# Block transposes for a third batch, later scores, and a new order of the opening, in a fused attention and two-FFN kernel

## The chip, the cores and the metric

The kernel runs on one core of a Trainium2 chip. Its metric is the device time of one execution in microseconds. A run of the kernel before took 1285.98 us in the median of three (1285.95 to 1286.9). The profiled execution is another one, and took 1288.85 us.

## The reference

```
scores = x @ state.T / 8        # per batch (8) and head (8); x 512 x 64, state 32 x 64
xread  = softmax(scores) @ state
scores2 = state @ x.T / 8
sread  = softmax(scores2) @ x
x  = concat(xread, sread)       # 544 tokens a batch, 512 wide, heads side by side
h  = relu(x @ w_in);  y = (h * h) @ w_out          # 512 -> 2048 -> 512
out = ((y @ w1) * (y @ w2)) @ w3 @ w_out2          # 512 -> 1024 -> 1024 -> 512
```

x and state come as float32, the six weights as float64 words, and the output is float32 (4352 x 512). The two softmaxes run over different axes of the same 512 x 32 scores.

## The kernel before

All large products run in float32r. Each operand is kept as a rounded high part and the rest (HI, LO; `split`, L80 to L85: the high part by ScalarE, the rest by a VectorE subtraction), and a product is three matmuls, `PASSES`. The weights are converted from float64 words by integer work: `convert64` (L132) is five VectorE instructions of 128 x 512 and one of ScalarE. A raw weight tile is one of three buffers (`raw`, L110) and is loaded three conversions ahead; `conv()` (L557) converts the next one and loads another.

xread @ w_in is computed as a product with state @ w_in: `make_sw(b, fg)` (L408) multiplies the state of batch b by a group of four 128-column blocks of w_in, by sixteen narrow matmuls into two banks. An h tile (c, f) (`h_tile`, L434) is then six matmuls of `sw` and the transposed softmax `aT`, and `y_tile` (L469), called two steps later, multiplies the squared tile by w_out, twelve matmuls into four banks y0 to y3 that stay open over a segment of f. At a segment's end the four banks are copied out and stored (L485 to L490).

The main loop (L631) steps through 16 f for each of 8 batches c, and then the state rows (c = 8). For c = 0 and 1 the steps are interleaved in segments of f (0 to 3 of batch 0, 0 to 3 of batch 1, 4 to 7 of batch 0, and so on). A step, with index i, is called a slot here. In slot i, h_tile is followed by the jobs of `side[i]` (conversions, loads, `make_sw`), a y_tile, and the jobs of `late[i]` (attention of a later batch). These lists are written by hand. Within them the planner of the language orders each engine's instructions by their place in the program and by when it reckons that their inputs are there. `tc.issue_after(ins)` keeps what a block issues on the engine of `ins`, and on no other engine, behind `ins`.

Attention of batch b (`att_steps`, L267) needs x twice: with d on the partitions for the scores (`xT`), and as it is for sread (`X`). For b < `BLK` (3), `load_x` and `make_x` load and copy X, `xpose` turns it by sixteen TensorE transposes, and `soft1a` and `a_T` turn scores and softmax by eight transposes each into banks of the pool `bank_m`, which has two buffers. For b >= BLK, `load_xb` (L240) loads x in pieces of 32 floats by eight DMAs for each half g, `turn_x` (L253) turns 32 x 32 blocks on VectorE, `soft1a` and `a_T` do the same with scores and softmax, and `load_xn` (L260) loads X. These batches hold a raw tile from `load_xb` to `turn_x`, and their output rows are in another order (L887). `att_slots` (L389) says in which of the 16 slots of the batch before each step of the attention comes.

The opening (L513 to L542) loads state and x, turns x, computes scores and softmax of batch 0, converts the first half of w_in's first group and makes `sw` and `aT` of batch 0. Its last step is `first`, the VectorE subtraction that ends the split of the second `aT`. The jobs of `side[0]` that VectorE does are issued behind it.

Of the kernel before, what the change touches and what calls it, by code (L numbers as in the profile page):

```python
# [8 lines left out]
F32 = mybir.dt.float32  # L9
# [3 lines left out]
ACTF = mybir.ActivationFunctionType  # L13
# [7 lines left out]
def kernel(  # L21
# [17 lines left out]
    nc = tc.nc  # L39
# [6 lines left out]
    P = 128  # L46
    G = 2
    HG = H // G
    J = S // P
    NF = DF // P  # L50
# [3 lines left out]
    NT9 = B * NS  # L54
    scale = 1.0 / float(D) ** 0.5
    HI, LO = 0, 1
    BLK = 3

    def f32(ap):
        return ap.bitcast(F32)  # L60
# [1 line left out]
    const = ctx.enter_context(tc.tile_pool(name="const", bufs=1))  # L62
# [6 lines left out]
    ebias = const.tile([P, 1], F32, name="ebias")  # L69
    nc.vector.memset(ebias, -896.0 * 2.0**23)  # L70
    def bank_m(name):
        return psum.tile([P, 512], F32, tag="m", bufs=2, name=name)
# [4 lines left out]
    def bank_y(d, name):  # L77
        return psum.tile([P, 512], F32, tag=f"y{d}", bufs=1, name=name)
# [88 lines left out]
    def load_win0(half, kk, early):  # L167

        cols = slice(half * 256, (half + 1) * 256)
        load64(("win0", half, kk), [w_in[k * P:(k + 1) * P, cols] for k in (2 * kk, 2 * kk + 1)], early)  # L170

    def make_win0(half, kk):
        if win_t[0] is None:
            win_t[0] = wpool.tile([P, ND, 512], F32, tag="wi0", bufs=2, name="win0")
        convert64(("win0", half, kk), win_t[0][:, 2 * kk:2 * kk + 2, half * 256:(half + 1) * 256])
# [10 lines left out]
    def make_wout(f):  # L186
        w = att.tile([P, 512], F32, tag="cw", bufs=2, name="cw")
        convert64(("wo", f), w)

        def halves():  # L190
            t = wpool.tile([P, 2, DM], F32R, tag="wo", bufs=NF, name=f"wo{f}")
            split(t[:, HI], t[:, LO], w)
            wo_t[f] = t

        open_splits.append(halves)
# [24 lines left out]
    def load_x(b, g, early=False):  # L220
        t = raw_tile(early, f"x{b}_{g}").bitcast(F32).rearrange("p a b -> p (a b)")
        nc.sync.dma_start(
            t.rearrange("p (h k) -> p h k", h=HG),
            x[b, g * HG:(g + 1) * HG].rearrange("h (p j) d -> p h (j d)", j=J),
        )
        raws["x", b, g] = t.rearrange("p (h j d) -> p j h d", h=HG, j=J)

    def make_x(b, g, engine, early=False):

        pool, tag, bufs = (wpool, "wo", NF) if early else (att, "X", 2)  # L230
        t = pool.tile([P, J, HG, D], F32, tag=tag, bufs=bufs, name=f"X{b}_{g}")
        if engine is nc.scalar:
            nc.scalar.copy(t, raws.pop(("x", b, g)))
        else:
            engine.tensor_copy(t, raws.pop(("x", b, g)))
        X[b, g] = t
# [30 lines left out]
    def att_steps(b):  # L267
# [45 lines left out]
        def soft1a(r):  # L313
            e = att.tile([P, J * HG, NS], F32, tag="e2" if b == 0 and r else "e1", bufs=1, name="e1")
            if b >= BLK:
                nc.vector.transpose(out=e.rearrange("p k n -> p (k n)"), in_=v["S", r])
# [20 lines left out]
        def a_T(r):  # L337
            e = v["e1", r].rearrange("p k n -> p (k n)")
            if b >= BLK:
                ps = v["S", r]  # L340
                nc.vector.transpose(out=ps, in_=e)
            else:
                ps = bank_m("ps_a")
                for j in range(J):
                    nc.tensor.transpose(ps[:, j * P:(j + 1) * P], e[:, j * P:(j + 1) * P], ident)
            t = pa.tile([P, 2, 512], F32R, tag=f"aT{r}", bufs=2, name=f"aT{r}")
            aT_t[b, r] = t
            return split(t[:, HI], t[:, LO], ps)
# [40 lines left out]
    def att_slots(b):  # L389
        if b >= B:  # L390
            return [[] for _ in range(NF)]
        xp, sc, s2, s1a, s1b, at, a2t, sr, srt = att_steps(b)
        if b >= BLK:
            return [
                [sc], [], [s2[0], s1a[0]], [],
                [s1b[0], s2[1]], [a2t[0]], [at[0], s1a[1]], [sr[0]],
                [s1b[1], srt[0]], [a2t[1]], [at[1]], [sr[1]], [srt[1]], [], [], [],
            ]
        return [
            [xp[0]], [xp[1]], [xp[2]], [xp[3]],  # L400
            [sc], [s2[0]], [a2t[0]], [s1a[0], s2[1]],
            [sr[0], s1b[0]], [srt[0]], [a2t[1], at[0]], [sr[1], s1a[1]],
            [srt[1], s1b[1]], [at[1]], [], [],
        ]

    SW = {}

    def make_sw(b, fg, cols=slice(0, 512)):  # L408
        pss = [bank_m("ps_sw") for _ in range(G)]
        for k in range(HG):  # L410
            for r in range(G):
                rows = slice(r * D, (r + 1) * D)
                nc.tensor.matmul(  # L413
                    pss[r][k * NS:(k + 1) * NS, cols], stT[rows, b, k, :], win_t[fg][rows, k, cols],
                    start=True, stop=True, tile_position=(r * D, k * NS),
                )
        for r in range(G):
            if (b, fg, r) not in SW:
                SW[b, fg, r] = pa.tile([P, 2, 512], F32R, tag=f"sw{r}", bufs=2, name=f"sw{r}")
            t = SW[b, fg, r]  # L420
            split(t[:, HI, cols], t[:, LO, cols], pss[r][:, cols])
# [73 lines left out]
    def load_st(half):  # L495

        t = raw_tile(True, f"st{half}").bitcast(F32).rearrange("p a b -> p (a b)")[:, :B * D]
        t = t.rearrange("p (b r d) -> p b r d", r=2, d=D)
        for k in range(HG):
            for r in range(G):  # L500
                (nc.sync if half else nc.scalar).dma_start(
                    t[k * NS:(k + 1) * NS, :, r, :],
                    state[half * (B // 2):(half + 1) * (B // 2), 2 * k + r].rearrange("b n d -> n b d"),
                )
        st.append(t.rearrange("p b r d -> p b (r d)"))

    def make_st(half):
        ps = bank_m("ps_st")
        for k in range(4):
            nc.tensor.transpose(ps[:, k * P:(k + 1) * P], st[half][:, k, :], ident)  # L510
        nc.scalar.copy(stT[:, 4 * half:4 * half + 4].rearrange("p b k n -> p (b k n)"), ps)

    load_st(0)  # L513
    load_x(0, 0, True)
    load_x(0, 1, True)
    load_win0(0, 0, True)
    make_x(0, 0, nc.vector)
    make_x(0, 1, nc.scalar)
    load_win0(0, 1, True)
    load_win0(1, 0, True)  # L520
    load_win0(1, 1, True)
    load_wout(0, True)
    for g in range(G):
        load_x(1, g, True)
    load_st(1)
    for g in range(G):
        make_x(1, g, nc.scalar, True)
    make_st(0)
    xp, sc, s2, s1a, s1b, at, a2t, sr, srt = att_steps(0)
    xp1, sc1, s21, s1a1, s1b1, at1, a2t1, sr1, srt1 = att_steps(1)  # L530
    for step in xp:
        step()
    sc()
    make_win0(0, 0)
    make_win0(0, 1)
# [2 lines left out]
    s1b[0]()  # L538
    at[0]()
    s1b[1]()  # L540
    make_sw(0, 0, slice(0, 256))
    first = at[1]()  # L542

    convs = [("win", 1, k) for k in range(ND)] + [("wo", f) for f in range(4, 8)]
    convs += [("win", 2, k) for k in range(ND)] + [("wo", f) for f in (8, 9)]
# [25 lines left out]
    def sw(b, fg):  # L571
        return lambda: make_sw(b, fg)

    side = {i: [] for i in range(NF * B)}
    late = {}
    side[0] = [lambda: make_win0(1, 0), s2[0], lambda: make_win0(1, 1), xp1[0], xp1[1], a2t[0]]
    side[1] = [lambda: make_sw(0, 0, slice(256, 512)), lambda: make_wout(0), xp1[2], xp1[3], sr[0], s2[1], sc1]
    side[2] = [conv, s1a1[0], srt[0], a2t[1], s1b1[0], sr[1], at1[0]]
    side[3] = [conv, s21[0], srt[1], s1a1[1], a2t1[0], conv, s1b1[1], sw(1, 0), at1[1]]
    side[4] = [conv, s21[1], sr1[0], lambda: make_st(1)]  # L580
    side[5] = [conv, a2t1[1], srt1[0]]
    side[6] = [conv, conv, sr1[1]]
# [7 lines left out]
    for b in range(2, B):  # L590
        for i, steps in enumerate(att_slots(b)):
            late[(b - 1) * NF + i] = steps
        for fg in range(NFG):
            if (b, fg) != (B - 1, NFG - 1):
                side[b * NF + 4 * fg + 1].append(sw(*((b, fg + 1) if fg + 1 < NFG else (b + 1, 0))))
        for g in range(G):
            i = 9 + g if b == 2 else (b - 2) * NF + 12 + g
            if b < BLK:
                side[i].append(lambda b=b, g=g: (load_x(b, g), make_x(b, g, nc.scalar)))
            else:  # L600
                side[i - 4].append(lambda b=b, g=g: load_xb(b, g))
                side[i - 2].append(lambda b=b, g=g: turn_x(b, g))
                side[i + 2].append(lambda b=b, g=g: load_xn(b, g))
# [266 lines left out]
    def out_tile(c, t, s):  # L870
# [15 lines left out]
        if c < B:  # L886
            rows_t = "(p j) e -> j p e" if c < BLK else "(j p) e -> j p e"  # L887
            dst = out[c * T:c * T + S, :].rearrange(rows_t, j=J)[t]
# [97 lines left out]
```

## Time and profile before

| what | value |
|---|---|
| profiled execution | 1288.85 us |
| span, first to last instruction | 1287.0 us |
| TensorE busy | 1253.1 us, 97% |
| VectorE busy | 798.0 us, 62% |
| ScalarE busy | 655.1 us, 51% |
| mean granted TensorE clock | 0.993 |
| TensorE granted half clock | 22.13 to 32.38 and 39.20 to 46.03 us |

Busy is the share of the span in which an engine has an instruction under way. The ends of matmuls are modelled, so a TensorE that waits a little between matmuls can be shown as busy; the spacing of the h tiles shows this better. PE is TensorE, DVE VectorE, ACT ScalarE, SP the engine that issues nearly all DMAs; SPq and ACTq are their issue queues.

### The profile page before, as it was taken

What the parts mean: (1) busy time and instruction counts of PE and PEld (TensorE: products, weight loads), DVE (VectorE), ACT (ScalarE), POOL (GpSimd) and SP (SyncE); (2) the same over time, 40 slices, a digit from 0 to 9 for tenths busy, and PEclk for the clock granted to TensorE, in tenths of its full rate; (3) what the DMA queues carried; (4) which work ended last, traced back from release to release, by engine and by line L of the source; (5) the groups of instructions that cost most, each with busy time, mean ns of one, the idle gap of its engine ahead of it and who ended that gap; (6) DMA issues with size and microseconds to landing.
All of it is one profiled execution on the core that took longest, in us unless ns stands there. A gap on an engine that the chain in (4) does not pass through costs nothing.

```text
span 1287.0 us, 16895 instructions
## 1 busy us (share of the span) xinstructions
PE 1253.1 (97%) x6392; PEld 986.7 (77%) x6392; DVE 798.0 (62%) x1444; ACT 655.1 (51%) x1174; POOL 23.3 (2%) x22
## 2 busy tenths in 40 slices
PE   4899999999999999999999999999999999999998
PEld 2566677677777777777789888888888888778877
DVE  4998965868577575753243763746465656666652
ACT  4776765657566565655555543535353442424231
POOL 0000000000000000000000000000510000000000
PEclk8899999999999999999999999999999999999999
DMA  6146525454453634510222531021530415050323
GB/s 212 43 151 202 179 80 118 105 123 144 95 163 76 162 114 113 151 49 34 73 91 66 174 108 46 37 95 61 172 116 29 154 59 178 27 188 26 106 66 99
DMA packets 122962, 137.94 MB, mean 107 GB/s; under 512 B 71425, under 2 KB 75009, under 8 KB 122369
## 3 DMA queue, kind: packets, MB, share of 16 engines
q1 hardware_dynamic: 121728, 136.61, 35.0%
q8 instruction: 50, 0.82, 0.3%
q10 hardware_dynamic: 1152, 0.26, 0.1%
q14 instruction: 32, 0.25, 0.1%
HBM read 93.32 MB, written 43.52 MB: 106 GB/s over the span
## 4 chain that ended last, share of the span: by engine, by line
PE 88%; DMA 4%; DVE 3%; ACT 3%; issue 1%; SPq 0%; ACTq 0%; DVEq 0%
PE y L480 26%; PE po L876 14%; PE qa L795 10%; PE qd L795 7%; PE qc L795 3%; PE ps_w L680 3%; PE qe L795 3%; PE ps_sw L413 2%; DMA yscr<-yo 2%; PE ab L850 2%; PE ps_r L362 1%; DMA x<-in_x_dram 1%; PE ps_s L290 1%; DVE sw L85 1%; PE ps_w L665 1%
## 5 line engine op out<-in xcount | busy, mean ns | idle before, releaser
L480 PE MATMUL y<-ghl,wo 128*128 128x512 f32 (+1 forms) x1728 | 406.6, 381 | 3.2 <-DVE yo L487 1.5
L480 PEld LDWEIGHTS y<-ghl,wo 128*128 128x128 f32 x1728 | 308.5, 188 | 93.9 <-ACT r L428 18.4
L85 DVE TENSOR_TENSOR ghl<-r,ghl 128x512 fp32r<-128x512 f32 (+1 forms) x144 | 94.9, 659 | 162.1 <-ACT ghl L84 161.2
L795 PE MATMUL qa<-yq,wq 128*128 128x512 f32 x576 | 146.3, 390 | 0.7 <-ACT s L803 0.7
L795 PEld LDWEIGHTS qa<-yq,wq 128*128 128x128 f32 x576 | 107.6, 188 | 24.8 <-ACT s L803 1.8
L803 ACT COPY s<-qa 128x512 f32<-128x512 f32 x96 | 56.1, 587 | 138.3 <-PE qa L795 127.4
L795 PE MATMUL qd<-yq,wq 128*128 128x512 f32 x384 | 98.3, 390 | 0.0
L876 PE MATMUL po<-w34b,c 128*128 128x512 f32 x408 | 95.8, 391 | 0.3 <-DVE o L885 0.3
L876 PE MATMUL po<-w,c 128*128 128x512 f32 x408 | 95.2, 390 | 0.0
L876 PEld LDWEIGHTS po<-w34b,c 128*128 128x128 f32 x408 | 75.7, 188 | 18.1 <-DVE c L85 1.0
L430 ACT ACTIVATE r<-r 128x512 f32<-128x512 f32 (+1 forms) x144 | 87.5, 608 | 3.2
L876 PEld LDWEIGHTS po<-w,c 128*128 128x128 f32 x408 | 75.6, 188 | 17.3 <-DVE c L85 0.8
L84 ACT CAST ghl<-r 128x512 fp32r<-128x512 f32 (+1 forms) x144 | 85.8, 596 | 3.8 <-PE y L480 0.5
L795 PEld LDWEIGHTS qd<-yq,wq 128*128 128x128 f32 x384 | 71.8, 188 | 15.7 <-ACT s L803 1.0
L129 ACT ACTIVATE ce<-ce,ebias 128x512 int32<-128x512 int32 x72 | 52.1, 725 | 48.5 <-DVE ce L128 48.4
L807 DVE TENSOR_TENSOR s<-qa,s 128x512 f32<-128x512 f32 x32 | 22.1, 691 | 75.2 <-ACT s L803 75.2
L84 ACT CAST c<-s 128x512 fp32r<-128x512 f32 x64 | 39.6, 621 | 37.1 <-DVE s L824 36.7
L84 ACT CAST yq<-yraw 128x512 fp32r<-128x512 f32 x70 | 42.6, 622 | 24.6 <-DVE yraw L770 15.5
L885 DVE TENSOR_TENSOR o<-po,opart 128x512 f32<-128x512 f32 x34 | 23.3, 688 | 45.4 <-PE po L876 34.5
L85 DVE TENSOR_TENSOR yq<-yraw,yq 128x512 fp32r<-128x512 f32 x70 | 46.6, 682 | 5.4 <-ACT yq L84 5.1
L795 PE MATMUL qc<-yq,wq 128*128 128x512 f32 x192 | 49.5, 390 | 0.0
L152 DVE SCALAR_TENSOR_TENSOR ce<-raw,ce 128x512 int32<-128x512 int32 x72 | 49.1, 683 | 0.3 <-ACT ce L129 0.3
(548 smaller groups left out, 1812.4 us busy)
## 6 DMA issues: line engine op xcount, KB each, us to landing
raw<-in_moe_w_dram SPq DMA_DIRECT2D x32, 512.0 KB, 4.6
yraw<-yscr SPq DMA_DIRECT2D x56, 256.0 KB, 5.3
raw<-in_moe_w_out_dram SPq DMA_DIRECT2D x24, 512.0 KB, 4.0
yscr<-yo SPq DMA_DIRECT2D x48, 256.0 KB, 3.0
oscr<-o SPq DMA_DIRECT2D x34, 256.0 KB, 2.2
opart<-oscr SPq DMA_DIRECT2D x34, 256.0 KB, 3.2
out_dram<-o SPq DMA_DIRECT2D x32, 256.0 KB, 3.0
raw<-in_moe_w_in_dram SPq DMA_DIRECT2D x12, 512.0 KB, 3.9
```

The lines of the kernel that those rows point to most:

```text
L84: nc.scalar.copy(hi, src)
L85: return nc.vector.tensor_tensor(out=lo, in0=src, in1=f32(hi), op=ALU.subtract)
L129: nc.scalar.activation(e, e, ACTF.Relu, bias=ebias, scale=8.0)
L152: nc.vector.scalar_tensor_tensor(out=e, in0=hw, scalar=-(2**31), in1=e, op0=ALU.bitwise_and, op1=ALU.bitwise_or)
L413: nc.tensor.matmul(pss[r][k * NS:(k + 1) * NS, cols], stT[rows, b, k, :], win_t[fg][rows, k, cols], start=True, stop=True, tile_position=( ...
L430: nc.scalar.activation(r[:, :n], r[:, :n], ACTF.Square)
L480: nc.tensor.matmul(y_ps[c, d][:, :n], wo_t[f][:, wi, d * P:(d + 1) * P], t[:, gi, :n], start=(f == f0 and k == 0), stop=(f == f1 - 1 and k ...
L680: nc.tensor.matmul(ps, t[:, wi, (j % 4) * P:(j % 4 + 1) * P], wo2_t[j][:, vi, :], start=(j == 0 and k == 0), stop=(j == N1 - 1 and k == 2),)
L795: nc.tensor.matmul(ps, W[w, kt][:, wi, m * P:(m + 1) * P], Y[v, kt][:, vi, :], start=(first and kt == 0 and k == 0), stop=(last and kt == ...
L803: nc.scalar.copy(t, ps)
L850: nc.tensor.matmul(pss[i][:, :NT9], w[:, wi, m * P:(m + 1) * P], Y[B, d][:, vi, :NT9], start=(d == 0 and k == 0), stop=(d == ND - 1 and k ...
L876: nc.tensor.matmul(ps, v[:, vi, t * P:(t + 1) * P], w[:, wi, :], start=(m == 0 and k == 0), stop=(m == QM - 1 and k == 2),)
```

## The change

- `BLK` goes from 3 to 2, so batch 2 goes by block turns, too. Its blocks are loaded in slots 14 and 15, turned in 16 and 17, and X is loaded in 20 and 21 (before: load and copy in 9 and 10).
- For b >= BLK the scores move from the first of the 16 slots to the third, the steps behind them by one slot.
- In the opening all loads go by SP, in the order x of batch 0, a pair of weight loads, half of the state, the rest. A small exponential at the start (`warm`) needs nothing that is loaded. Both halves of x are copied by VectorE, and the state is turned behind x.
- The softmax's `a_T` of batch 0 and the first `make_sw` take banks of the y group instead of `bank_m`.
- The copies of batch 1's x (`make_x`, ScalarE) come behind `first` in the program, in an `issue_after(first.ins)` block.
- In `side[0]` to `side[3]`, `a2t[0]`, `sr[0]`, `srt[0]` and `sr[1]` come later, and `s2[0]` behind both conversions.

```diff
-    BLK = 3
+    BLK = 2
...
-                ps = bank_m("ps_a")
+                ps = bank_m("ps_a") if b else bank_y(2 + r, "ps_a")
...
-                [sc], [], [s2[0], s1a[0]], [],
-                [s1b[0], s2[1]], [a2t[0]], [at[0], s1a[1]], [sr[0]],
-                [s1b[1], srt[0]], [a2t[1]], [at[1]], [sr[1]], [srt[1]], [], [], [],
+                [], [], [sc], [s2[0], s1a[0]],
+                [], [s1b[0], s2[1]], [a2t[0]], [at[0], s1a[1]], [sr[0]],
+                [s1b[1], srt[0]], [a2t[1]], [at[1]], [sr[1]], [srt[1]], [], [],
...
-    def make_sw(b, fg, cols=slice(0, 512)):
-        pss = [bank_m("ps_sw") for _ in range(G)]
+    def make_sw(b, fg, cols=slice(0, 512), banks=None):
+        pss = [banks(r, "ps_sw") if banks else bank_m("ps_sw") for r in range(G)]
...
-                (nc.sync if half else nc.scalar).dma_start(
+                nc.sync.dma_start(
...
+    warm = const.tile([P, 1], F32, name="warm")
+    nc.scalar.activation(warm, ebias, ACTF.Exp, scale=0.0)
+    for g in range(G):
+        load_x(0, g, True)
+    load_win0(0, 0, True)
     load_st(0)
-    load_x(0, 0, True)
-    load_x(0, 1, True)
-    load_win0(0, 0, True)
-    make_x(0, 0, nc.vector)
-    make_x(0, 1, nc.scalar)
     load_win0(0, 1, True)
+    for g in range(G):
+        make_x(0, g, nc.vector)
...
-    for g in range(G):
-        make_x(1, g, nc.scalar, True)
-    make_st(0)
...
     for step in xp:
         step()
+    make_st(0)
     sc()
...
-    make_sw(0, 0, slice(0, 256))
+    make_sw(0, 0, slice(0, 256), bank_y)
     first = at[1]()
+    with tc.issue_after(first.ins):
+        for g in range(G):
+            make_x(1, g, nc.scalar, True)
...
-    side[0] = [lambda: make_win0(1, 0), s2[0], lambda: make_win0(1, 1), xp1[0], xp1[1], a2t[0]]
-    side[1] = [lambda: make_sw(0, 0, slice(256, 512)), lambda: make_wout(0), xp1[2], xp1[3], sr[0], s2[1], sc1]
-    side[2] = [conv, s1a1[0], srt[0], a2t[1], s1b1[0], sr[1], at1[0]]
-    side[3] = [conv, s21[0], srt[1], s1a1[1], a2t1[0], conv, s1b1[1], sw(1, 0), at1[1]]
+    side[0] = [lambda: make_win0(1, 0), lambda: make_win0(1, 1), s2[0], xp1[0], xp1[1]]
+    side[1] = [lambda: make_sw(0, 0, slice(256, 512)), lambda: make_wout(0), xp1[2], xp1[3], a2t[0], s2[1], sc1]
+    side[2] = [conv, s1a1[0], sr[0], a2t[1], s1b1[0], srt[0], at1[0]]
+    side[3] = [conv, s21[0], sr[1], srt[1], s1a1[1], a2t1[0], conv, s1b1[1], sw(1, 0), at1[1]]
...
-            i = 9 + g if b == 2 else (b - 2) * NF + 12 + g
+            i = (b - 2) * NF + (18 if b == 2 else 12) + g
             if b < BLK:
                 side[i].append(lambda b=b, g=g: (load_x(b, g), make_x(b, g, nc.scalar)))
             else:
```

The lines behind the `else` are unchanged: `load_xb` in slot i - 4, `turn_x` in i - 2, `load_xn` in i + 2.

## Rows read from the trace of the kernel before

**Rows 1.** The page, part 1: busy us (share of the span) xinstructions.

```profile
PE 1253.1 (97%) x6392; PEld 986.7 (77%) x6392; DVE 798.0 (62%) x1444; ACT 655.1 (51%) x1174; POOL 23.3 (2%) x22
```

**Rows 2.** Windows, the first 10 us: busy us (x) by engine, clock, DMA share, GB/s.

```profile
0.00:10.00 10.00, 0.00 (x0) 0.00 (x0) 0.75 (x2) 1.79 (x2) 0.70 (x6) 1.00 0.83 238
```

**Rows 3.** Timeline, opening: start us, us, engine, line, operation [idle before, releaser].

```profile
0.74 7.43 ACTq L501 DMA_DIRECT2D st<-in_state_dram  x8
0.74 0.40 SPq L121 DMA_DIRECT2D raw<-in_moe_w_out_dram  x1
...
6.90 0.69 DVE L235 COPY X<-x 128x1024 f32<-128x1024 f32 x1 [6.04 <-DMA x<-in_x_dram]
8.20 1.28 ACT L233 ACT_TABLE_LOAD   x1 [8.20 <-DMA st<-in_state_dram]
...
11.06 1.09 PE L510 MATMUL ps_st<-ident,st 128*128 128x128 f32 x4 [11.06 <-DMA raw<-in_moe_w_in_dram]
...
15.60 1.83 PE L290 MATMUL ps_s<-xT,stT 64*32 64x512 f32 x16
...
20.66 1.04 ACT L233 COPY X<-x 128x1024 f32<-128x1024 f32 x1 [2.08 <-DMA x<-in_x_dram]
...
25.30 0.69 DVE L335 TENSOR_TENSOR e<-e,sm 128x512 f32<-128x512 f32 x1
...
28.64 1.11 PE L345 MATMUL ps_a<-ident,e 128*128 128x128 f32 x4
...
30.41 0.69 DVE L85 TENSOR_TENSOR aT<-ps_a,aT 128x512 fp32r<-128x512 f32 x1 [0.81 <-ACT aT L84]
```

**Rows 4.** Windows, slots 1 to 25 and parts of them, columns as above.

```profile
31.10:174.93 143.83, 136.57 (x732) 95.36 (x731) 130.44 (x272) 104.57 (x187) 0.00 (x0) 0.97 0.45 136
...
31.10:47.95 16.85, 12.63 (x82) 8.03 (x82) 14.38 (x36) 12.32 (x25) 0.00 (x0) 0.76 0.00 1
...
39.20:46.03 6.83, 6.06 (x35) 4.25 (x35) 5.12 (x12) 4.13 (x10) 0.00 (x0) 0.50 0.00 1
...
119.27:144.63 25.36, 25.05 (x115) 17.88 (x114) 23.89 (x46) 18.54 (x33) 0.00 (x0) 1.00 0.71 214
```

**Rows 5.** Line 442, h tiles 13, 14, 63 to 65: ns, first to last start.

```profile
L442 PE MATMUL ph__1129<-aT,sw x6: 388/389/389, 109.2 to 110.3; 128*128 128x512 f32 x6
L442 PE MATMUL ph__1192<-aT,sw x6: 387/394/496, 116.9 to 119.3; 128*128 128x512 f32 x6
...
L442 PE MATMUL ph__3484<-aT,sw x6: 389/389/389, 360.1 to 361.2; 128*128 128x512 f32 x6
L442 PE MATMUL ph__3511<-aT,sw x6: 389/389/389, 364.1 to 365.3; 128*128 128x512 f32 x6
L442 PE MATMUL ph__3562<-aT,sw x6: 387/397/496, 369.3 to 370.6; 128*128 128x512 f32 x6
```

**Rows 6.** Timeline of TensorE before h tile 36.

```profile
226.92 1.57 PE L413 MATMUL ps_sw<-win,stT 64*32 64x512 f32 x16 [0.71 <-ACT S L296]
...
229.68 0.50 PE L442 MATMUL ph__2265<-aT,sw 128*128 128x512 f32 x1 [1.18 <-ACT sw L84]
```

**Rows 7.** Waits of TensorE, whole span: us in total, times, longest us.

```profile
PE ps_a L353 <- ACT e L310: 3.4, 1, 3.4
...
PE y L480 <- ACT yo L489: 1.4, 5, 0.3
```

**Rows 8.** VectorE's block transposes, 205 to 365 us (by line); TensorE's transposes (timeline).

```profile
L257 DVE STREAM_TRANSPOSE xT<-xb 128x512 f32<-128x512 f32 x12 | 8.2, 699 | 0.1
...
183.87 0.60 PE L353 MATMUL ps_a<-ident,e 128*128 128x128 f32 x4
184.31 0.60 PE L345 MATMUL ps_a<-ident,e 128*128 128x128 f32 x4
```

**Rows 9.** Timeline of SP, block loads of batch 3; SP's waits for them, whole span.

```profile
202.15 12.76 SPq L247 DMA_DIRECT2D xb<-in_x_dram  x16
...
SPq L247 <- DVE cm L149: 40.9, 6, 10.0
```

## The prediction, on record before the changed kernel ran

> **What bounds the kernel now.** I read the page's busy shares first: TensorE is busy for 97% of the span, VectorE for 62% [rows 1]. TensorE therefore sets the end, and a change gains only what it takes out of TensorE's work or out of its waits. The windows come next: in the first 10 us TensorE does nothing, while the DMA engines move 238 GB/s [rows 2]. The timeline of the opening says why. The state's eight loads stand on ScalarE's queue until 8.2 us, so the copy of the second half of batch 0's x (L233) starts only after its table load, at 9.48, and TensorE starts at 11.06 with the state's transposes. Scores start at 15.60, the softmax's last multiply ends at 25.99, and the split of the second aT, which the kernel calls `first`, ends at 31.10 [rows 3].
>
> Then VectorE is the partner that is hard to outrun: between 31.10 and 174.93 us (slots 1 to 25; a slot is one pass of the h/y loop, counted from 0) it is busy 130.44 of 143.83 us, because it converts the float64 weights [rows 4]. The rows of the h tiles tell what a slot costs: from the last matmul of one tile to the last of the next a plain slot takes 365.3 - 361.2 = 4.1 us, and one with sixteen narrow matmuls more 5.3. Slot 14 takes 119.3 - 110.3 = 9.0 us with the work of a 5.3 us slot, so 3.7 us of it are waits that the busy share hides [rows 5]. Behind slot 25 such losses are few. One is at 226.92 to 229.68, where TensorE idles 0.71 and 1.18 us because the state-weight product of slot 33 queues for a bank that batch 3's scores hold [rows 6]. The table of TensorE's waits adds 1.4 us in five waits for y evacuations at batch turns [rows 7].
>
> **Part 1, the opening up to `first`.** Removed: the eight issues on ScalarE, the table load from the path (the dummy Exp brings it into idle time at the start), one ScalarE copy of 1.04 us (VectorE does it, as it did its twin in 0.69 at 6.90), and the wait of x's transposes behind the state's. Added: eight issues on SP in front of the second weight pair. SP's line up to the state is then x, x, one weight pair, state. By 11.06 us the two queues together had brought a weight load that stands at the head of SP (0.5 MB, [rows 3]), x (1.0), a weight pair (0.5) and the state (0.25). If that weight load stays at the head, as the planner has it now, the state lands as late as before; if it doesn't, 0.5 MB at 238 GB/s are 2.1 us less. x's own transposes are through by then, so scores follow 1.09 us of state transposes and a copy of some 0.6. That gives a start between 12.9 and 10.8 with 0.2 for the handovers; I take 12.4, a gain of 3.2 (bounds 2.7 and 4.8).
>
> From scores to `first` it took 15.5 us. Two waits in that go. (a) ScalarE stood 2.08 us for the DMA of batch 1's x, and the first exponential ran behind that copy of 1.04 us, at 20.66 to 21.70, when its input was there: 1.0 us [rows 3]. (b) The second aT's transposes came at 28.64, 2.65 us after their input at 25.99, since the same two banks carried ps_n, ps_sw and ps_a; with banks of the idle y group they can run at once. Together 3.65; I take 3.3, since VectorE may find two `sw` splits in its line. The sum is -6.5, from -2.65 (only the banks help) to -8.4.
>
> The fence round batch 1's copies is one doubt. `issue_after` queues only what the block issues on the named instruction's own engine; `first` is a VectorE subtraction and the copies are ScalarE's, so it holds back nothing. Only their later place in program order does.
>
> **Part 2, from `first` to the end of slot 2 (31.10 to 47.95).** VectorE is busy 14.38 of 16.85 us there and the clock is at its lower level (0.50 of full, 1.2 GHz) from 39.20 to 46.03, after TensorE waited 3.4 us for the scaled exponentials of batch 0 [rows 4, 7]. The change puts that a2 transpose one slot later and both weight conversions before the first state softmax, so the 3.4 us wait leaves. I count -2.0: VectorE's line stays the bound there, and the a2 work (a transpose and sixteen small matmuls) must be done later. Bounds 0 and -3.4.
>
> **Part 3, slots 3 to 19.** Batch 2's x leaves slots 9 and 10 (two loads in raw tiles that conversions need, two ScalarE copies); slot 14's 3.7 us stand right behind these, so up to -3.7 is to be had. In exchange slots 14 to 17 get sixteen block loads and four VectorE transposes of 0.70 us, 2.8 in all [rows 8]. Between 119.27 and 144.63 VectorE is already busy 23.89 of 25.36 us [rows 4]: no cover is left, so I charge 2.8 us in full, and as much of the 3.7 as VectorE's share of idle allows, 1.8. Term: +1.0. The bad end is set by SP. Two blocks took it 12.76 us of line time at slots 30 to 33 [rows 9], and every weight load and y store behind them waits; half of that would be +6.4. The good end is -3.7.
>
> **Part 4, TensorE's own work.** Batch 2 loses 16 transposes of x, 8 of the scores and 8 of aT. Four of them take 184.31 - 183.87 = 0.44 us [rows 8], so 32 take 3.5. They lie in slots 17 to 30, where TensorE sets the pace except for slot 19; I take -3.0 (bounds 0 and -3.5). VectorE's two transposes per r (four of 0.70 = 2.8 us) lie mostly in slots 19 to 27, which have room. ScalarE loses four PSUM copies and two x copies. The plain copy of x comes by two loads of 0.5 MB in slots 20 and 21 instead; SP's line holds no weight loads that are near due there, so they cost nothing, and at worst a plain slot.
>
> The Trainium skill (VectorE: DVE Perf Modes, Rules for kernel authors) advises TensorE for full transposes and VectorE for 32 x 32 ones. By that advice this part would gain nothing; by the busy shares [rows 1] the busier engine gives work to the less busy one. The advice holds for an engine with room.
>
> **Part 5, scores two slots later.** For batch 3 the product of slot 33 now comes ahead of the scores and finds its banks free: -1.9 [rows 6], bounds 0 and -3.0 (the work behind it restarts late, too). The scores themselves wait for block loads that land no sooner; 13 slots are used instead of 12 of 16, and h of the next batch waits for none of it. For batches 4 to 7 the score copies leave the slots in which y banks are emptied: half of the 1.4 us of [rows 7], -0.7, bounds 0 and -1.4.
>
> **The sum.** -6.5 - 2.0 + 1.0 - 3.0 - 1.9 - 0.7 = -13.1. The profiled execution took 1288.85 us, a span of 1287.0 and 1.85 around it, so it would come to 1275.8. It stands 2.9 above the median of the three runs, 1285.98, and I carry the difference over: 1272.9, rounded 1273. All bounds at their good ends give -23.4, at their bad ends +3.7.
>
> **Rivals.**
> (A) The fence holds nothing. The planner puts batch 1's copies before the exponentials or aT's casts again, ScalarE waits for loads that land past 20 us, and part 1 gains the banks alone, -2.65. For it: the fence's engine, and the 1.04 us copy at 20.66. Against: their later place. Sum -9.3, 1277.
> (B) The small pieces. Block loads move 128-byte pieces, and slots 16 to 19 already use 0.71 of the DMA engines' time [rows 4]; two blocks of 0.5 MB in 12.76 us are 82 GB/s against 238 [rows 2, 9]. Weight loads come late and conversions with them: part 3 at its bad end, +6.4. Sum -7.7, 1278. The Trainium skill (DMA: Bandwidth & Descriptors, Specifications) speaks for it: pieces under 512 bytes miss the line rate. By that rule the loads cost the engines more than their bytes, as the 82 GB/s agree.
> (C) SP stands still, the slower side. A block load waits in SP's line for a raw tile that a conversion must free; weight loads and y stores queue behind it. Blocks of later batches have waited up to 10.0 us at once for this [rows 9], when conversions were few. Two such waits in slots 14 to 17, where conversions feed TensorE, cost 20: part 3 turns from +1.0 to +20 and part 5 keeps its gain: +5.9, 1292. It decides from 14 us of waits upward. Against it: conversions come once or twice a slot there, so raw tiles come free every 4 us.
> (D) All VectorE time follows. An earlier start shifts its whole stream, the waits of slot 14 and its like vanish, and the clock stays up: parts 1 to 3 at -8.4 - 3.4 - 3.7, sum -21.1, 1265.
>
> **Chances.** Forecast 0.40, A 0.20, B 0.15, C 0.12, D 0.13. Within 0.2% (2.6 us, about what this kernel's timing can tell from none) falls a part of B and of C, 0.05 and 0.02; slower is the rest of C, 0.10; faster by more is 0.83. The range goes from 1263 (beyond D's 1265) to 1283 (beyond B, with room for unknown order from the planner). The forecast's own range is 1268 to 1277.
>
> **What would show it.** `first` ending near 24.6 instead of 31.10; no table load behind 2 us; the second aT transposes within 0.5 us of their input; ScalarE's copies of batch 1 behind the second aT (fence or place works) or ahead of it (A). h of slot 14 within 6 us. The SP waits of block loads in slots 14 to 17 short (else C), DMA share there below 0.9 (else B). No TensorE wait for ps_sw behind S copies near slot 36, and five y waits at batch turns shorter. TensorE matmuls 32 fewer. The prediction is wrong if `first` moves by under 3 us, or if slots 14 to 19 take over 5 us longer than before.

## The result and the profile after

The changed kernel takes 1298.7 us in the median of four runs (1296.8 to 1302.3), beside 1286.3 for the kernel before on the same chip: 1.0097 times as long, with an interval from 1.0085 to 1.0109. It is 12.4 us slower, and 26 above the forecast. Its profiled execution took 1299.85 us, with a span of 1297.7.

The page, part 1, stands against [rows 1]:

```profile
PE 1260.5 (97%) x6360; PEld 986.8 (76%) x6360; DVE 807.2 (62%) x1453; ACT 651.6 (50%) x1168; POOL 21.8 (2%) x22
```

The 32 transposes are gone from TensorE (6392 to 6360 matmuls), and yet it is shown busy for 7.4 us more. That isn't more work: it is gaps between matmuls that the busy share hides, and matmuls at the lower clock (the mean granted clock is 0.991, before 0.993).

Timeline of the opening, ScalarE and VectorE, against [rows 3]:

```profile
0.73 1.28 ACT L514 ACT_TABLE_LOAD   x1 [0.73 <-PEq L974]
...
8.46 0.72 ACT L129 ACTIVATE ce<-ce,ebias 128x512 int32<-128x512 int32 x1 [6.23 <-DVE ce L128]
9.09 1.05 ACT L282 COPY xT<-ps_x 128x512 f32<-128x512 f32 x2
...
20.52 1.99 ACT L233 COPY X<-x 128x1024 f32<-128x1024 f32 x2
...
24.81 0.59 ACT L84 CAST aT<-ps_a 128x512 fp32r<-128x512 f32 x1 [0.31 <-PE ps_a L345]
...
25.43 0.69 DVE L85 TENSOR_TENSOR aT<-ps_a,aT 128x512 fp32r<-128x512 f32 x1 [0.20 <-ACT aT L84]
```

`first` ends at 26.12 where it ended at 31.10: the opening is 5.0 us shorter. The last matmul of h in slot 2 starts at 41.64 (before: 47.95). The new opening leads by 6.3 us there, of 8.5 forecast. (This depends on the profile: in the profiles with the old opening this matmul starts between 46.2 and 47.9, with the new opening and the new order of jobs between 39.5 and 42.6.) The next table follows this lead: the start of the last h matmul in a slot, in us, read from the rows of the h tiles as in [rows 5].

| slot | before | after | opening alone | batch 2's blocks alone | blocks in own tiles |
|---|---|---|---|---|---|
| 3 | 54.38 | 47.78 | 46.13 | 52.98 | 45.64 |
| 8 | 86.90 | 82.80 | 81.72 | 85.50 | 80.67 |
| 19 | 144.63 | 136.17 | 138.62 | 138.94 | 132.63 |
| 23 | 165.00 | 165.13 | 158.97 | 170.32 | 156.69 |
| 31 | 205.91 | 211.96 | 201.50 | 215.80 | 196.62 |
| 64 | 365.27 | 371.15 | 360.84 | 376.85 | 355.86 |
| 127 | 658.99 | 668.33 | 654.54 | 670.67 | 649.90 |

The profiles of before and of blocks in own tiles lie 2.6 above and 2.6 below their kernels' medians, the one of the opening alone 2.7 below, so differences of columns are read for where they arise, and sizes are taken from the medians. Up to slot 19 the changed kernel is 8.5 us ahead. By slot 23 it has lost all of that, and by slot 31 it is 6 behind. The h tiles of slots 18 to 20, 22, 23 and 28 after (L442, ns, first to last start) show where the steps are:

```profile
L442 PE MATMUL ph__1387<-aT,sw x6: 388/389/389, 129.4 to 130.5; 128*128 128x512 f32 x6
...
L442 PE MATMUL ph__1467<-aT,sw x6: 389/389/389, 135.0 to 136.2; 128*128 128x512 f32 x6
...
L442 PE MATMUL ph__1522<-aT,sw x6: 389/394/797, 141.7 to 145.9; 128*128 128x512 f32 x6
...
L442 PE MATMUL ph__1637<-aT,sw x6: 388/389/389, 147.3 to 148.4; 128*128 128x512 f32 x6
...
L442 PE MATMUL ph__1697<-aT,sw x6: 389/389/389, 161.3 to 165.1; 128*128 128x512 f32 x6
...
L442 PE MATMUL ph__1924<-aT,sw x6: 389/390/478, 186.0 to 197.1; 128*128 128x512 f32 x6
```

Slot 20 takes 9.7 us. Slots 21 and 22 take 1.1 and 1.4, because their y work is left undone, and slot 23 takes 16.7 with that work in it; together slots 20 to 23 take 28.9 us where they took 20.4. Slot 28 takes 11.4, again with y work that had piled up. VectorE's and TensorE's timelines in that place give the reason:

```profile
138.50 0.69 DVE L152 SCALAR_TENSOR_TENSOR ce<-raw,ce 128x512 int32<-128x512 int32 x1 [1.58 <-ACT ce L129]
139.22 0.69 DVE L155 SCALAR_TENSOR_TENSOR win<-cm,ce 128x512 f32<-128x512 f32 x1
141.66 1.29 DVE L85 TENSOR_TENSOR sw<-ps_sw,sw 128x512 fp32r<-128x512 f32 x2 [1.75 <-ACT sw L84]
142.87 1.30 DVE L257 STREAM_TRANSPOSE xT<-xb 128x512 f32<-128x512 f32 x2
150.46 0.69 DVE L301 TENSOR_REDUCE nm<-S 128x1 f32<-128x512 f32 x1 [6.30 <-ACT S L296]
151.07 0.42 DVE L128 TENSOR_SCALAR ce<-raw 128x512 int32<-128x512 int32 x1
```

```profile
139.97 1.05 PE L413 MATMUL ps_sw<-win,stT 64*32 64x512 f32 x4 [2.05 <-DVE win L155]
...
148.71 1.06 PE L290 MATMUL ps_s<-xT,stT 64*32 64x512 f32 x8
150.48 1.57 PE L413 MATMUL ps_sw<-win,stT 64*32 64x512 f32 x16 [0.71 <-ACT S L296]
154.09 1.23 PE L480 MATMUL y<-ghl,wo 128*128 128x512 f32 x4 [2.03 <-ACT yo L489]
```

One thing follows from the other: TensorE waits for a piece of w_in that is converted late, VectorE then waits for the product, turns batch 2's second block only then, and stands 6.30 us for the scores of that block, while weights for y are converted only from 151.07 on. In that last wait weights are not missing: two loads of w_out had been issued from 136.74 on, the second by 139.56, and loads of weights issued between 136 and 152 us landed within 4.9 us. They stay unconverted because their instructions stand behind the maximum (L301) in VectorE's order. The SP timeline shows what came before:

```profile
121.83 0.33 SPq L121 DMA_DIRECT2D raw<-in_moe_w_in_dram  x1
125.51 4.96 SPq L247 DMA_DIRECT2D xb<-in_x_dram  x8
130.57 0.43 SPq L121 DMA_DIRECT2D raw<-in_moe_w_in_dram  x1
131.34 5.31 SPq L247 DMA_DIRECT2D xb<-in_x_dram  x8
136.74 2.82 SPq L121 DMA_DIRECT2D raw<-in_moe_w_out_dram  x2
```

Between 121.83 and 136.74 one weight load of half a megabyte is issued, behind eight block loads. The first block holds its raw buffer from 125.51 to the end of its turn at 134.80, the second from 131.34 to 144.17. Windows of 120 to 170 us, before and after (us, then busy time of PE, PEld, DVE, ACT, POOL, clock, DMA share, GB/s):

```profile
120.00:170.00 50.00, 49.69 (x252) 36.38 (x251) 47.22 (x93) 38.92 (x70) 0.00 (x0) 1.00 0.57 171
```

```profile
120.00:170.00 50.00, 43.07 (x190) 28.38 (x189) 37.94 (x72) 27.90 (x50) 0.00 (x0) 0.93 0.51 136
```

VectorE idles 12.1 of 50 us where it idled 2.8; 6.3 of the 12.1 are the wait for the scores. The clock falls a little too (0.93 in the mean, 0.83 from 140 to 160 us), after TensorE's waits. The DMA engines are less busy than before, so they are not the limit.

### The profile page after: what moved, and what is told of

Same layout as the page of the kernel before. It is cut to its first block, busy times and chain, and to the rows that moved or that the text cites. A ratio compares the mean times of both kernels' runs of the same rounds, so it can differ in the third digit from the quotient of the medians.

```text
span 1297.7 us, 16874 instructions
## 1 busy us (share of the span) xinstructions
PE 1260.5 (97%) x6360; PEld 986.8 (76%) x6360; DVE 807.2 (62%) x1453; ACT 651.6 (50%) x1168; POOL 21.8 (2%) x22
## 4 chain that ended last, share of the span: by engine, by line
PE 88%; DVE 5%; DMA 3%; ACT 3%; issue 1%; SPq 0%; DVEq 0%; ACTq 0%
PE y L480 26%; PE po L879 12%; PE qa L798 10%; PE qd L798 7%; PE qc L798 3%; PE ps_w L683 3%; PE qe L798 3%; PE ps_sw L413 2%; PE ab L853 2%; DMA yscr<-yo 1%; PE ps_r L362 1%; PE ps_s L290 1%; DMA wraw<-w12s 1%; DVE yq L85 1%; PE ps_a L353 1%
## 5 line engine op out<-in xcount | busy, mean ns | idle before, releaser
L129 ACT ACTIVATE ce<-ce,ebias 128x512 int32<-128x512 int32 x72 | 52.0, 722 | 42.7 <-DVE ce L128 42.6
L413 PE MATMUL ps_sw<-win,stT 64*32 64x512 f32 (+1 forms) x528 | 46.3, 598 | 8.2 <-DVE win L155 6.4
L84 ACT CAST yq<-yraw 128x512 fp32r<-128x512 f32 x70 | 42.6, 623 | 22.4 <-DVE yraw L773 15.4
```

The lines of the kernel that those rows point to most:

```text
L84: nc.scalar.copy(hi, src)
L129: nc.scalar.activation(e, e, ACTF.Relu, bias=ebias, scale=8.0)
L413: nc.tensor.matmul(pss[r][k * NS:(k + 1) * NS, cols], stT[rows, b, k, :], win_t[fg][rows, k, cols], start=True, stop=True, tile_position=( ...
```

## The experiments

A ratio is to the kernel before on the same chip, with its interval; a time is a median. On the chips used the kernel before has medians of 1286.0 to 1287.0 us, so a difference of two times can be off by 1 us where the chips differ.

**The three parts alone.** `e1_no_blocks2` takes batch 2's part out of the changed kernel.

```diff
-    BLK = 2
+    BLK = 3
-            i = (b - 2) * NF + (18 if b == 2 else 12) + g
+            i = 9 + g if b == 2 else (b - 2) * NF + 12 + g
```

> The changed kernel without its batch 2 part (BLK back at 3, batch 2's x loaded in slots 9 and 10, old attention slots for batch 2); opening and later scores stay. Theory T (batch 2's block loads in slots 14 and 15 hold two of three raw buffers, conversions starve, VectorE stands 6.3 us for the scores): all of the loss between slots 19 and 28 goes, the opening's gain of about 6 us stays, the batch turns cost about 1: 1279 to 1282. Rival R (the earlier opening brings slots 14 to 28 ahead of the weights, with or without blocks): the loss stays for the most part, 1288 or more.

1286.4 us, 1.0002 (0.9993 to 1.0011). The loss goes, as T has it, but the time is above T's range: the opening's gain is not kept.

`e2_blocks2_alone` is the same edit the other way round, in the kernel before, with the new slots for batch 2's attention alone.

> The kernel before with the batch 2 part alone (BLK 2, its loads and its attention slots; batches 3 to 7 and the opening as before). T: a loss of 14 to 18 us in slots 19 to 28, less 3.5 us of TensorE transposes: 1297 to 1303. R: without the earlier opening the stream of weights is in time, 1284 to 1289.

1299.8 us, 1.0098 (1.0085 to 1.0111). Batch 2's blocks alone make the whole loss, without any help from the opening. R falls for this part.

`e3_opening_alone` is the changed kernel without the blocks and with the old attention slots; `e4_scores_alone` has only the new list in `att_slots`.

> The kernel before with the new opening alone (loads by SP, banks, copies, order of slots 0 to 3). T: first and slot 3 about 6 us earlier, and it is kept: 1279 to 1281. R: the gain is given back in slots 14 to 28: 1285 to 1288.

> The kernel before with the later scores alone (batches 3 to 7). T: the waits round slot 36 shrink from 3.9 to about 3.3 us, and each of five batch turns costs 0.2 to 0.5 us more: 1286 to 1288. Rival (the prediction's own terms, -1.9 and -0.7): 1283.5.

Opening alone: 1286.0 us, 0.9994 (0.9983 to 1.0005); later scores alone: 1286.1, 0.9996 (0.9987 to 1.0005). Neither can be told from no change. For the opening that is R's range (T is missed), but not R's place: at slot 31 its profile still leads by 4.4 us. The later scores come out as T has it. The opening's runs reach from 1282.8 to 1290.1, twice the spread of the kernel before; the profiled one in the table above is among the fastest.

**What makes batch 2's blocks dear.** Four edits of the changed kernel.

`e5_blocks_own_tile` puts the blocks where nothing else is before slot 20.

```diff
-        t = raw_tile(False, f"xb{b}_{g}").bitcast(F32).rearrange("p a b -> p (a b)")
+        if b == 2:
+            t = att.tile([P, HG, J, D], F32, tag="X", bufs=2, name=f"xb{b}_{g}").rearrange("p h j d -> p (h j d)")
+        else:
+            t = raw_tile(False, f"xb{b}_{g}").bitcast(F32).rearrange("p a b -> p (a b)")
```

> The changed kernel (1298.7 us), with batch 2's blocks loaded into the two X buffers, which stand empty until slot 20, and not into raw buffers. The planner can then spread the block loads over slots 5 to 13. Theory T1 (the blocks hold two of three raw buffers from 125 to 144 us, conversions run on one, and that is the loss of 12.4): the losses of slots 20 to 28 fall from 16 to under 4 us, 1284 to 1288. Rival T2 (SP's line and the 64 KB loads): they pass through the same line, only earlier, 1293 or more. Rival T4 (VectorE's order puts the maximum of batch 2's scores ahead of the next conversions and stands 6.3 us for it): the maximum still waits for turned x, a gain of at most half, 1292 to 1296.

1283.9 us, 0.9978 (0.9967 to 0.9989): 14.8 less than the changed kernel, and less than before; T2 and T4 as they were put fall. In its window VectorE idles 0.7 us:

```profile
120.00:170.00 50.00, 49.65 (x254) 33.01 (x252) 49.32 (x99) 37.24 (x66) 0.00 (x0) 1.00 0.55 158
```

Since nothing holds them back there, the block loads go out one to four at a time between weight loads, from 49.56 us on:

```profile
55.44 0.35 SPq L121 DMA_DIRECT2D raw<-in_moe_w_in_dram  x1
55.83 1.50 SPq L250 DMA_DIRECT2D xb<-in_x_dram  x3
62.01 0.35 SPq L121 DMA_DIRECT2D raw<-in_moe_w_in_dram  x1
62.40 0.96 SPq L250 DMA_DIRECT2D xb<-in_x_dram  x2
```

So this edit frees two raw buffers and takes the bursts off SP's line at once.

`e6_blocks_by_gpsimd`: `(nc.gpsimd if b == 2 else nc.sync).dma_start(...)` for the block loads.

> The changed kernel with batch 2's sixteen block loads issued by GpSimd and not by SP; they still go into raw buffers. T2 (SP's line: 11 us of block loads between 125.5 and 136.7 hold the weight loads behind them): 1286 to 1290. T1 and T4: the raw buffers and the order on VectorE are as they were, 1295 to 1300.

1292.7 us, 1.0052 (1.0032 to 1.0071): half of the loss. It lies between the ranges of T2 and of T1 and T4. The blocks now hold their buffers longer than in the changed kernel (some 18 us for the first; until 159.77, some 26, for the second), and still VectorE is busy for 43.19 us of the window, not 37.94; T1 alone, with the buffers as the whole price, does not hold. The Trainium skill (DMA: Bandwidth & Descriptors, Issuing engines are not separate DMA queues) says that issuing from another engine only saves the issuing sequencer's time, which is usually small beside the DMA itself. Here that time was 10.3 us of SP's line in the row above, in front of weight loads; the gain of 6.0 does not measure it cleanly, because the planner also put conversions ahead of the maximum, which now waits 1.30 us and not 6.30:

```profile
161.99 0.69 DVE L301 TENSOR_REDUCE nm<-S 128x1 f32<-128x512 f32 x1 [1.30 <-ACT S L296]
```

`e7_att2_two_later` gives batch 2 a list of its own, in which each step stands two slots later.

> The changed kernel with all attention steps of batch 2 two slots later (scores in slot 20), loads and turns as they were. T4: the wait of 6.3 us on VectorE goes, and conversions run on: 1289 to 1293. T1: conversions still lack raw buffers, 1295 to 1299.

1297.5 us, 1.0087 (1.0072 to 1.0102). This was to take the wait for the scores away, and did not: the planner left the maximum where it was among VectorE's instructions, and it waits 6.76 us:

```profile
150.88 0.69 DVE L301 TENSOR_REDUCE nm<-S 128x1 f32<-128x512 f32 x1 [6.76 <-ACT S L296]
```

T4 is therefore not tested by it. What it shows is that the slot in the list does not set the place on the engine.

`e8_plain_loads` loads batch 2's x in one piece for each half (so its scores are of x in another order, and its output is not the reference's).

```diff
+        if b == 2:
+            nc.sync.dma_start(t.rearrange("p (h j d) -> p h j d", h=HG, j=J), x[b, g * HG:(g + 1) * HG].rearrange("h (j p) d -> p h j d", p=P))
+            raws["xb", b, g] = t
+            return
```

> The changed kernel with batch 2's sixteen loads of 64 KB in pieces of 128 bytes replaced by two loads of 512 KB with 256-byte pieces into the same raw buffers in the same slots (batch 2's scores are then of x in another order). T3 (small pieces and their issues): 1286 to 1290. T1: the buffers are held nearly as long, since the turns stay in slots 16 and 17: 1293 to 1298.

1289.9 us, 1.0023 (1.0012 to 1.0033): 8.8 of 12.4 come back, as T3 has it. The loads land in 4.1 us (median), each block holds its buffer for 6 us and not 9 to 13, the maximum waits for nothing, and VectorE is busy for 46.84 us of the window.

Together: the price of batch 2's blocks in raw buffers is VectorE standing still in the stretch where it sets the pace (e1, e2 and e5 show the price, the windows the standing still). Three things enter it: SP's line, the raw buffers, and the place of the maximum in VectorE's order. The wait of the maximum goes along with the loss: 6.30 us in the changed kernel, 7.44 in e2 and 6.76 in e7, which lose 11 to 13 us; 1.30 in e6; none in e8 and e5. The time that the buffers are held doesn't (e6 holds them longest). Since each edit also moved that order, how the price divides among the three stays open: no run kept the buffers and moved only the maximum, or gave the ring a fourth buffer.

**Where the opening's gain goes.** In `e9_own_tile_stores`, `e10_before_stores` and `e11_opening_stores` (the kernel of e5, the kernel before, the opening alone) the third and fourth y copy at a batch's end need not wait for the store of the first two:

```diff
-                o = pa.tile([P, 512], F32, tag="yo", bufs=2, name="yo")
+                if f1 == NF and c < 7 and d >= 2:
+                    o = att.tile([P, 512], F32, tag="cw", bufs=2, name="yo")
+                else:
+                    o = pa.tile([P, 512], F32, tag="yo", bufs=2, name="yo")
```

> The changed kernel with batch 2's blocks in the X buffers (1283.9 us) and, at the end of a batch, the third and fourth y copy in the two cw buffers, so that no copy waits for the store of the first or second (which took 2.0 to 4.5 us to land). Theory S (these stores' waits cost 0.7 us a batch turn and up to 4 where a store is slow, and make the runs differ by 6 us): 1278 to 1281, and a spread under 4 us. Rival (TensorE has other work at the turns, or the cw buffers hold back conversions): 1283 to 1286.

> The kernel before with the cw buffers for the third and fourth y copy. S: 0.6 to 0.8 us at each of seven batch turns and 0.5 at slot 27: 1282 to 1284. Rival: 1286 to 1288.

> The new opening alone with the cw buffers for the third and fourth y copy. Theory S for the opening (it keeps 4 to 5 us up to slot 26, and slow stores at slot 27 take them back in most runs): 4 to 5 us less than the kernel before with the same buffers, 1278 to 1280. Rival V (the opening's gain is lost on VectorE between slots 3 and 8, whatever the stores): 1 to 2 us less, 1281 to 1283.

1275.7 us, 0.9920 (0.9907 to 0.9932), with a spread of 1.7; 1283.0, 0.9972 (0.9961 to 0.9983); 1281.1, 0.9961 (0.9948 to 0.9975). The waits for stores are real (S holds for e10, and e9 gains more than S had) and the spread shrinks, but the opening is worth 1.9 us beside its twin, not 4 to 5: V is nearer. Windows from slot 3 to slot 8 of e10 and of e11 show it:

```profile
52.64:85.17 32.53, 32.35 (x182) 21.19 (x181) 29.81 (x67) 22.57 (x41) 0.00 (x0) 1.00 0.38 130
```

```profile
47.60:84.18 36.58, 34.79 (x199) 22.14 (x197) 32.30 (x73) 23.24 (x42) 0.00 (x0) 1.00 0.36 121
```

The opening starts this stretch 5.0 us earlier and ends it 1.0 earlier. VectorE has 2.5 us more to do in it (73 instructions for 67), and idles 1.6 longer. So a good part of the lead at slot 3 is VectorE work that was put behind slot 3.

`e12_opening_old_jobs` has the opening with the lists `side[0]` to `side[3]` of before.

> The new opening alone (1286.0 us), with the jobs of slots 0 to 3 in their order of before, the work on batch 0's state rows one slot earlier again. Prediction's view: the wait of 3.4 us for the scaled exponentials returns in slot 2, 1287 to 1289. Rival V (the later work only moves VectorE's load from slot 2 to slot 4, which lost 1.3 us more): the same, 1285 to 1287.

1284.3 us, 0.9983 (0.9974 to 0.9992). The old order is no worse, and by its median 1.7 better (1.4 by the two ratios, whose intervals overlap). The wait for the scaled exponentials did return on TensorE:

```profile
PE ps_a L353 <- ACT e L310: 4.3, 1, 4.3
```

Yet the time did not grow: with the old order the stretch from slot 3 to slot 8 starts later (49.2 us; e3: 46.1) but takes 32.1 us, with the new one 35.6 (e3). The prediction's -2.0 for the reordering was not there at the end.

In `e13_all_stores`, `e14_before_all_stores`, `e15_opening_all_stores` and `e16_all_stores_old_jobs` (e13 with the old lists) the copies at the earlier segment ends go to the xT buffers, too:

```diff
+                elif f1 < NF and d >= 2:
+                    o = att.tile([P, 512], F32, tag="xT", bufs=4, name="yo")
```

> The kernel with batch 2's blocks in the X buffers and late stores in cw (1275.7 us), and in the segments that end in slots 5 to 15 the third and fourth y copy in the xT buffers, which are empty there. Theory W (waits for y stores at these ends stand VectorE for 1 to 2 us each): 1271 to 1274. Rival V (VectorE's work alone sets the pace there): 1275 to 1276.

> The kernel before with the cw and the xT buffers for the third and fourth y copy. W: 1279 to 1281. V: 1282 to 1284.

> The new opening alone with the cw and the xT buffers for the third and fourth y copy. W: the opening is worth 3.5 to 5 us against the kernel before with the same buffers. V: 2 us or less, as with the cw buffers alone.

> The kernel with own tiles and all stores' buffers, and the jobs of slots 0 to 3 in their order of before. If the later work on batch 0's state rows costs what the opening gained (1.7 us between the two openings alone): 1.5 to 2 us below the kernel with the new order. If only the waits for stores made that difference: the same within 0.7.

1278.5 us (0.9940, 0.9925 to 0.9955), 1282.0 (0.9966, 0.9953 to 0.9978), 1279.6 (0.9945, 0.9932 to 0.9957) and 1274.9 (0.9912, 0.9899 to 0.9926). The opening is now worth 2.5 us, hardly more than 1.9. W holds for a small part at most, and e13 is slower than e9, against both theories; why stays open. e16 is 3.6 us below e13, more than either of its theories had.

`e17_best_old_jobs` is e9 with the old lists; `e18_copies_first` adds to it that the first exponents on ScalarE stand behind the copies of x turned (`xpose` returns its copy):

```diff
     for step in xp:
-        step()
+        last = step()
     make_st(0)
     sc()
-    make_win0(0, 0)
-    make_win0(0, 1)
+    with tc.issue_after(last.ins):
+        make_win0(0, 0)
+        make_win0(0, 1)
```

> The kernel with batch 2's blocks in the X buffers and the late stores in cw (1275.7 us), with the jobs of slots 0 to 3 in their order of before. If that order costs what the kernels with all buffers showed (3.6 us): 1271 to 1273. If that difference came from the buffers in xT alone: 1275 to 1276.5.

> The kernel e17 with the exponents of the first two weight loads held behind the last copy of x turned on ScalarE. If ScalarE's order keeps the scores late: they start 1.5 to 2 us earlier, first ends 1 to 2 us earlier, and the time falls by 0.5 to 2 us. Rival: the product with w_in, whose exponents are now later, is late instead, and first stands where it was or later: 0 to 1 us more.

1276.3 us (0.9922, 0.9909 to 0.9936) and 1275.3 (0.9914, 0.9901 to 0.9928). The order of the jobs makes no difference here; the 3.6 us of e16 came only with the xT buffers. In e18 the scores start at 11.31 and not 13.26, and `first` ends at 24.07 and not 25.81, as expected; part of that is that its score matmuls ran faster (last section). The time falls by 1.0, which the intervals don't tell from none. The next wait is rival A's, on ScalarE:

```profile
20.67 1.04 ACT L233 COPY X<-x 128x1024 f32<-128x1024 f32 x1 [1.04 <-DMA x<-in_x_dram]
21.62 0.58 ACT L285 COPY xT<-ps_x 128x512 f32<-128x512 f32 x1
22.10 1.25 ACT L84 CAST aT<-ps_a 128x512 fp32r<-128x512 f32 x2
```

The casts of aT stand behind the copy of batch 1's x, which waits for its load. The intervals of e9, e16, e17 and e18 overlap. By their medians these four beat both kernels, by 10 to 11 us the one before and by 22 to 24 the changed one.

## Why the prediction was wrong

**Part 3, the step that failed.** The prediction charged 2.8 us of VectorE time for the turns and gave 1.8 back, +1.0, with +6.4 as the bad end from half of SP's line time [rows 9]. Batch 2's part alone costs 12.6 us (e2) and includes what part 4 gains; the same part in own tiles gains 2.5 (e5 against e1; 3.1 by the ratios). The difference of 15 us is the misjudged price. The prediction did see that no cover is left on VectorE [rows 4], but priced the work on VectorE and put its standing still at nothing: in the window from 120 to 170 us VectorE idles 9.3 us more, and 6.3 us of its idle time are one wait, that for batch 2's scores, which no part, rival or sign of the prediction names. Part 4 also took it that TensorE sets the pace in slots 17 to 30 but for slot 19; before the change VectorE was busy for 27.8 of the 30 us from 140 to 170 (slots 19 to 24), so there was no cover there either.

**Rival C came nearest,** with the right place (raw buffers, SP's line, weights behind) and the wrong mechanism in detail. It looked for block loads that wait for a raw tile. They waited little (second line); weight loads waited more (first line), but they did so before, too (25.3 us in the largest such row). SP's waits over 110 to 200 us after:

```profile
SPq L121 <- DVE ce L152: 26.8, 7, 9.4
...
SPq L247 <- DVE cm L146: 3.6, 1, 3.6
```

By the prediction's own signs C would have been ruled out, since these waits are short, and slots 14 to 19 took 30.2 us (106.01 to 136.17) where they took 34.3 before. Slot 14 itself fell from 9.0 us to 7.0, not to the 6 of the sign. The loss stands a few slots later, in 20 to 28, where no sign had been set. That C's total was nearest is in part luck: its 20 us were two long waits in slots 14 to 17, of which one of 3.6 us came. Chance 0.12 was too little for a step that lengthens the hold on three buffers which feed the pacing engine.

**Rival B** was wrong: the DMA share in the window falls to 0.51 (0.87 at most in ten of its us, from 130 to 140), and weight loads landed in 3.8 to 3.9 us in the median of the span, no later than before (3.9 to 4.0). **Rival D,** in which the opening's whole gain stays and more comes to it, was wrong: the opening alone leaves 0.8 to 2.5 us.

**Part 1 was right,** up to the speed of TensorE: `first` at 26.12, -5.0 of -6.5. The scores started at 13.29, not 12.4, because ScalarE's order put an exponent that waits for weights (8.46) ahead of the copies of x turned; with the copies first (e18) they start 2.0 us earlier. The rest depends on the execution: in the profiles of the same opening in which the score matmuls ran fast, `first` ended between 24.38 (e5) and 24.90 us (e3), where 24.6 was forecast (with the old opening it ended between 29.6 and 31.1). In e9 it ended at 24.52:

```profile
23.83 0.69 DVE L85 TENSOR_TENSOR aT<-ps_a,aT 128x512 fp32r<-128x512 f32 x1 [0.20 <-ACT aT L84]
```

The table load and the second aT went as forecast. Rival A's order came true (batch 1's copies run at 20.52, ahead of both aT casts), but they did not wait in this profile, and its price, part 1 cut to -2.65, did not come.

**Parts 1 and 2 were wrong as terms of the sum.** Up to slot 2 part 2 gave -1.3 of -2.0 (15.5 us from `first` for 16.85), but slot 4 then takes 16.3 us where it took 14.3 (and 14.8 in e12, with the old order): the work that was put later comes due there. And the prediction added -8.5 as if an earlier `first` were an earlier end. Of a lead of 5.0 (e11 against e10) to 8.3 us (e3) at slot 3, 0.8 (e3) to 2.5 us (e15) are left at the end. Between slots 3 and 8 go 4.0 us of the lead in e11, 3.1 in e3 and 2.4 in e15; there VectorE has the moved work to do and waits longer. That VectorE sets the pace there is read from the windows of e10 and e11; where the rest goes behind slot 8 is not shown.

**Part 4 can't be read by itself:** e5 against e1 gains 2.5 us, of -3.0 forecast, but this holds the turns of part 3 and the two loads and copies that leave slots 9 and 10, too. With more y copy buffers in both (e9 against e11, where later scores are in it as well) the difference is 5.3. Whether the advice of the Trainium skill (VectorE: DVE Perf Modes, Rules for kernel authors) to turn whole tiles on TensorE would have been better here is not shown: no run moves the transposes alone.

**Part 5 had the wait right and the sum wrong.** No `ps_sw` waits behind scores near slot 36. Later scores alone give 0.5 us (-0.6 to +1.7 within the interval), not 2.6. In the profiles slots 35 to 39 take 26.4 us in e4 and 27.3 before, so the waits of 1.9 us that went are worth 0.9 there. The y waits did not get shorter in the changed kernel: TensorE waits 7.9 us for y copies (longest 2.0), before 2.9. Where the rest went is not shown.

## What to carry to other kernels

Before adding a user to a ring of buffers that feeds the pacing engine, count how long it holds a buffer, what stands behind it in the issuing queue, and which instruction of that engine will wait for its result with ready work behind it. Charge the idle time of that engine, not the new instructions. Look for a buffer that is empty at that time first: here it turned a loss of 12 us into a gain of 2.8 (and spread the loads at the same time). An earlier start isn't an earlier end: work that is only put later comes due where the pacing engine has no room. And a wait on an engine that doesn't set the pace (the 4.3 us of e12) can come back without a price.

## What the hardware showed unexpectedly

The sixteen score matmuls of the opening took 1.96 us in the changed kernel and 1.09 in e9, from the same start, and the granted clock is shown as 1.00 in both windows (13 to 19 us):

```profile
13.29 1.96 PE L290 MATMUL ps_s<-xT,stT 64*32 64x512 f32 x16 [0.68 <-ACT stT L511]
```

```profile
13.31 1.09 PE L293 MATMUL ps_s<-xT,stT 64*32 64x512 f32 x16 [0.68 <-ACT stT L517]
```

Both values occur among profiles of the same opening (1.96 in nine, 1.09 in five; e18, whose opening differs, has 1.09), and move slot 0 by 1.5 to 2 us; what decides stays open. A y store (256 KB, four of 52 half that) took 1.7 to 5.4 us to land after the change (median 2.9), and with two copy buffers TensorE feels the long ones: at the turn of slot 83 it stood 2.05 us for one.
